# First heads of a decay attention loaded six tokens to a partition, two decay rows copied by the scalar engine, GpSimd's head constants in four steps, new constants of the planner

## The chip, the cores and the metric

The kernel runs on one core of one Trainium2 chip. The metric is device time in microseconds (us) of one execution, the median of several runs. A profiled execution of the kernel before, taken by the hardware profiler, gives the rows that are read below; its times count from the first instruction. The engines are named as the profile names them: PE (TensorE, matmuls), PEld (its weight loads), DVE (VectorE), ACT (ScalarE), POOL (GpSimd), SP (SyncE, which issues most DMAs). L903 is line 903 of the kernel before. In the changed kernel lines below the planner stand 5 to 20 lines further down, so that one statement has two numbers: L657 and L675 (scores), L763 and L781 (values), L903 and L921 (first MoE product), L804 and L822, L815 and L833 (the two matmul steps of a group's division).

## The reference

```python
# q, k, v: (8, 8, 576, 64); f: (8, 8, 576); all float32
scores = np.matmul(q, k.transpose(0, 1, 3, 2)) / np.sqrt(64)
cum = np.cumsum(np.log(np.clip(f, 1e-4, 1.0)), axis=-1)
scores = np.where(causal, -1e9, scores + cum[..., :, None] - cum[..., None, :])
attn = np.exp(scores - scores.max(-1, keepdims=True))
attn = attn / (attn.sum(-1, keepdims=True) + 1e-9)
x = np.matmul(attn, v).transpose(0, 2, 1, 3).reshape(8 * 576, 512)
h = np.maximum(np.maximum(x @ w1, x @ w2), x @ w3)      # 512 -> 768
out = h @ w_out                                        # 768 -> 512
```

## The kernel before

There are 64 heads, eight to a batch, and behind each batch the MoE product of its 576 tokens. The work of a head is cut into a unit 2 (queries 0 to 255) and a unit 1 (queries 256 to 575); for the first eight heads unit 1 is cut again into "a" and "b". Scores stand transposed, keys on partitions. `scores` (line 628) writes q times k and the causal mask into PSUM in a first pass (L657, L673), takes the maximum over keys with ACT and DVE (L712 to L724), across partitions with POOL (L727), lets POOL copy that row to where a matmul can use it (L734), subtracts it by a second pass of matmuls (L657 again) and lets ACT take the exponential (L742). `values` (line 752) multiplies by v and a column of ones (L763). For the first eight heads `finish_group` (line 790) divides four heads at once: PE turns the row sums (L804), DVE adds 1e-9 and takes the reciprocal (L819, L820), ACT widens them (L808), PE spreads them (L815). Later pairs of heads divide by way of two small DMAs through DRAM (`finish_pair`, line 863), and `split_x` makes the two parts of x that the MoE product needs (L877, L879). `gemm1` (L903) and `gemm2` (L932) are the MoE product in three fp32r products each; their weights are converted on the chip, 24 blocks, by ACT and DVE (`load_weights`, L511 to L521).

The first eight heads are prepared in another way than the rest. `load_raw` (line 459) loads a head's k and q, each as 96 partitions of six pieces of 64 numbers (256 bytes). `turn_head` (line 466) turns them by PE (L473) in two steps of three matmuls, and ACT and DVE copy the result out of PSUM into the tiles KF and QF (L479 to L482). Row 64 of KF holds the decays of the head's keys: `decay` (line 422) loads f, takes the logarithm and the running sum (L435), scales eight heads of it into a tile (L439), and ACT's queue issues one small DMA a head that puts one row into KF (L442). PE runs 20 matmuls on nothing (L455) beside this. When heads 0 to 3 are through, POOL writes constants into the tiles that the later heads use (`head_constants`, line 385, four memsets, one step for each of two buffers).

The order of all of it is worked out when the program is built, by a list scheduler (`Plan.emit`, line 86): every step has an engine, a cost and a priority, and each engine takes the ready step with the lowest rank, which is the step's priority less a share (`BLW`) of the work that hangs on it. Estimates of delays (`LAG`, `ROOM`, `LATE`, and `moved`, the time at which the queue of transfers is through) set when a step is ready; `LIKE` and `HOLD` say how far PE may go out of rank to put matmuls with 65 columns of weights behind a short one. What comes out is one fixed sequence for each engine, and on the chip each engine runs its own sequence in order, waiting at semaphores. The priorities are numbers at the end of the kernel function (lines 970 to 1051): `DP` for the decays, `DPW` for the weights' loads, `LEAD`, `UP`, `VO`, `FO`, `XO` for scores, values, division and split.

```python
add("POOL", 3300, lambda i=i: head_constants(i), w=[f"qs{i}", f"ks{i}"], prio=p)   # L1029
```

## Time and profile before

| | |
|---|---|
| median of 3 runs | 947.04 us (944.66, 947.04, 947.17) |
| the profiled execution, by the same clock | 944.31 us |
| its span, first to last instruction | 942.5 us |
| PE busy | 931.9 us (99%) |
| DVE, ACT, POOL busy | 641.0, 498.9, 249.8 us |
| mean granted clock of TensorE | 0.995 |

The span is 1.8 us shorter than the profiled execution's own time. A busy PE is not PE at its peak: a matmul counts as busy while it waits for its weights and while the clock is low. [...] "Idle before" in a row is the time in which that engine had nothing to do ahead of the row, with the instruction that ended the wait.

### The profile page before, as it was taken

How to read it: one execution, taken by the hardware profiler on the slowest of the kernel's cores; microseconds unless marked ns; L12 is line 12 of the kernel's file. 1: busy time of each engine (PE TensorE's matmuls, PEld its weight loads, DVE VectorE, ACT ScalarE, POOL GpSimd, SP SyncE). 2: the span in 40 equal slices, each digit the busy share in tenths (PEclk: the TensorE clock that was granted, in tenths of full speed). 3: DMA queues.
4: the chain of work that ended last, by engine and by line, in shares of the span. 5: the costliest groups of instructions: out<-in, count | busy, mean ns of one | idle time of the engine just before them, and what ended most of it. 6: DMA issues, size and time to landing. Idle time of an engine off the chain costs nothing.

```text
span 942.5 us, 18410 instructions
## 1 busy us (share of the span) xinstructions
PE 931.9 (99%) x6730; PEld 879.1 (93%) x6730; DVE 641.0 (68%) x1331; ACT 498.9 (53%) x1074; POOL 249.8 (27%) x313
## 2 busy tenths in 40 slices
PE   8999999999999999999999999999999999999998
PEld 6889988899989999999999999999999999999998
DVE  6998985567858686685967686686857776563311
ACT  5775754455555564555556564455655555453111
POOL 5663332322222221222122331222122321210000
PEclk9988999999999999999999999999999999999999
DMA  9776065546354354445445344545435454400000
GB/s 215 217 171 200 14 179 135 147 114 163 89 139 125 99 142 117 130 103 161 102 113 150 81 133 105 159 101 155 112 95 153 102 139 100 112 15 36 1 34 23
DMA packets 102826, 110.33 MB, mean 117 GB/s; under 512 B 60896, under 2 KB 70368, under 8 KB 102736
## 3 DMA queue, kind: packets, MB, share of 16 engines
q1 hardware_dynamic: 102480, 109.14, 44.7%
q8 instruction: 53, 0.87, 0.4%
q14 instruction: 37, 0.30, 0.1%
q10 hardware_dynamic: 256, 0.02, 0.0%
HBM read 49.56 MB, written 9.86 MB: 63 GB/s over the span
## 4 chain that ended last, share of the span: by engine, by line
PE 95%; DVE 2%; DMA 1%; ACT 1%; issue 0%; SPq 0%; ACTq 0%; DVEq 0%
PE mp L903 48%; PE mp L932 16%; PE t L763 15%; PE s L657 13%; DMA w<-in_moe_w_out_dram 1%; PE mp L473 0%; DMA qs<-u 0%; PE mp L657 0%; PE s L673 0%; SPq L578 0%; PE mp L763 0%; PE mp L815 0%; PE t L473 0%; PE t L815 0%; DVE w_r L521 0%
## 5 line engine op out<-in xcount | busy, mean ns | idle before, releaser
L903 PE MATMUL mp<-xh_r,w_r 128*128 128x320 f32 (+1 forms) x2160 | 466.4, 298 | 0.0
L903 PEld LDWEIGHTS mp<-xh_r,w_r 128*128 128x128 f32 x2160 | 357.2, 188 | 1.6 <-ACT tm L910 0.3
L903 PE MATMUL mp<-xl_r,w_r 128*128 128x320 f32 (+1 forms) x1080 | 319.5, 296 | 0.0
L727 POOL PARTITION_ALL_REDUCE gm<-mx x131 | 161.8, 1253 | 555.9 <-DVE mx L717 421.5
L903 PEld LDWEIGHTS mp<-xl_r,w_r 128*128 128x128 f32 x1080 | 203.3, 188 | 0.4
L912 DVE TENSOR_TENSOR tm<-mp,tm 128x256 f32<-128x256 f32 (+1 forms) x192 | 86.8, 452 | 87.1 <-PE mp L903 78.0
L742 ACT ACTIVATE pf<-s 128x384 f32<-128x384 f32 (+3 forms) x235 | 103.4, 508 | 53.7 <-PE s L657 48.4
L657 PE MATMUL s<-qs_r,ks_r 128*128 128x320 f32 (+4 forms) x784 | 123.7, 279 | 0.4 <-ACT hmh_r L915 0.4
L932 PE MATMUL mp<-w_r,hmh_r 128*128 128x512 f32 (+1 forms) x396 | 123.1, 393 | 0.0
L657 PEld LDWEIGHTS s<-qs_r,ks_r 128*128 128x128 f32 (+1 forms) x784 | 115.3, 181 | 5.3 <-ACT hmh_r L915 0.7
L749 DVE TENSOR_TENSOR pl_r<-pf,ph_r 128x1216 fp32r<-128x1216 f32 (+1 forms) x96 | 97.5, 1022 | 13.2 <-ACT ph_r L748 9.8
L717 DVE TENSOR_TENSOR mx<-mx,s 128x320 f32<-128x320 f32 (+3 forms) x248 | 92.1, 372 | 11.7 <-ACT mx L724 3.6
L748 ACT ACTIVATE ph_r<-pf 128x1216 fp32r<-128x1216 f32 (+1 forms) x96 | 83.0, 884 | 5.8 <-PE t L763 5.5
L915 ACT ACTIVATE hmh_r<-tm 128x256 fp32r<-128x256 f32 x96 | 39.7, 414 | 82.8 <-DVE tm L912 82.7
L932 PEld LDWEIGHTS mp<-w_r,hmh_r 128*128 128x128 f32 x396 | 70.3, 188 | 12.1
L534 DVE STREAM_TRANSPOSE hl<-hl 128x576 f32<-128x576 f32 x56 | 68.0, 1240 | 15.1 <-DMA hl<-in_k_dram 9.6
L932 PE MATMUL mp<-w_r,hml_r 128*128 128x512 f32 (+1 forms) x198 | 76.7, 387 | 0.0
L910 ACT ACTIVATE tm<-mp 128x256 f32<-128x256 f32 (+1 forms) x96 | 39.6, 413 | 59.1 <-PE mp L903 56.2
L917 DVE TENSOR_TENSOR hml_r<-tm,hmh_r 128x256 fp32r<-128x256 f32 x96 | 44.0, 458 | 24.7 <-ACT hmh_r L915 24.1
L734 POOL CAST qs_r<-gm 1x320 fp32r<-1x320 f32 (+1 forms) x112 | 56.0, 519 | 4.6
L763 PE MATMUL t<-ph_r,va_r 128*65 128x320 f32 (+4 forms) x336 | 52.7, 273 | 0.0
L763 PE MATMUL t<-ph_r,vl_r 128*65 128x320 f32 (+4 forms) x336 | 52.6, 273 | 0.0
(212 smaller groups left out, 1196.7 us busy)
## 6 DMA issues: line engine op xcount, KB each, us to landing
qs_r<-hl SPq DMA_DIRECT2D x168, 144.0 KB
ks_r<-hl SPq DMA_DIRECT2D x168, 144.0 KB
w<-in_moe_w_dram SPq DMA_DIRECT2D x18, 512.0 KB
out_dram<-o_r SPq DMA_DIRECT2D x35, 256.0 KB
hl<-in_q_dram SPq DMA_DIRECT2D x14, 576.0 KB
hl<-in_k_dram SPq DMA_DIRECT2D x14, 576.0 KB
r_r<-rdram SPq DMA_DIRECT2D x56, 144.0 KB
vn<-in_v_dram SPq DMA_DIRECT2D x50, 128.0 KB
```

Of the source, the lines that this page charges most:

```text
L534: add("DVE", 1085, lambda e=e, tt=tt, xs=xs: nc.vector.transpose(tt[:, e], xs[:, e]), [key + "0"], [key + "1"], prio)
L657: nc.tensor.matmul(bank[bk][0:l.shape[-1], col:col + w], l, rhs(qa, w), start=start and bk not in begun, stop=stop, skip_group_check=True)
L717: nc.vector.tensor_tensor(mt[:, a:a + w], mt[:, a:a + w], bank[bk][:, col:col + w], op=ALU.max)
L727: add("POOL", 450 + 2.6 * nq, lambda: nc.gpsimd.partition_all_reduce(gm, mt, P, bass.bass_isa.ReduceOp.max), [km, km + "a"], [kg], prio)
L734: add("POOL", 130 + 0.9 * nq, lambda: nc.gpsimd.tensor_copy(shift_row(), gm[row:row + 1, :]), [kg], [kx], prio)
L742: add("ACT", act_cost(w), lambda bk=bk, w=w, col=col: nc.scalar.activation((pg(unit) if pk else pf)[:, col:col + w], bank[bk][:, 0:w], AF. ...
L748: add("ACT", act_cost(PW[unit]) + 40, lambda: nc.scalar.activation(ph(unit), pf, AF.Copy), [fk], [hk], prio)
L749: add("DVE", dve_cost(PW[unit]), lambda: nc.vector.tensor_tensor(pl(unit), pf, ph(unit).bitcast(F32), op=ALU.subtract), [fk, hk], [lk], prio)
L763: nc.tensor.matmul(t[:D + 1, qa:qa + w], src()[:, j, c, :], pr()[:, col:col + w], start=first and x == 0, stop=last, skip_group_check=True,)
L903: nc.tensor.matmul(m, unit_w(i, fb)[:, w, kt, :], xx, start=kt == 0 and x == 0, stop=kt == KT - 1 and x == 2,)
L912: add("DVE", dve_cost(cn), lambda m=m: nc.vector.tensor_tensor(t, m, t, op=ALU.max), [km, kt_], [kt_], prio)
L932: nc.tensor.matmul(mp[:, 0:cn], l[:, fb, cs], unit_o(fb)[:, r, ds], start=fb == 0 and x == 0, stop=fb == FT - 1 and x == 2,)
```

## The change

Heads 0 to 7: a partition now takes six tokens that follow each other, so k and q are 96 pieces of 1,536 bytes each; a step of `turn_head` turns q alone or k alone, so q's can begin before k is there; the copies out of PSUM put the tokens back in order, writing every sixth number. f is loaded first of all, with head 1's row a second time on partition 64, and ACT copies the rows of heads 0 and 1 itself; six rows stay small DMAs. The first three blocks of weights are loaded ahead of heads 2 to 7. POOL's constants are eight steps. The maximum and what follows on DVE and POOL stand half a priority earlier (`CB`). The planner has one queue of transfers for all engines, a longer delay for ACT and DVE, and other priorities.

```diff
-    ROOM = {"PE": (0.93, 0), "ACT": (1.0, 0), "DVE": (1.0, 0), "POOL": (1.0, 450), "SP": (1.0, 0)}
-    LIKE, HOLD = 1.7, 1.0
+    ROOM = {"PE": (0.93, 0), "ACT": (1.0, 0), "DVE": (1.0, 60), "POOL": (1.0, 450), "SP": (1.0, 0)}
+    MORE = (0, 150, 0, 0, 0)
+    LIKE, HOLD = 3.0, 0.55
...
-    def head_constants(i):
-        nc.gpsimd.memset(KS(i)[:, :, S:SP].bitcast(F32), 0.0)
...
+    def head_constants(i, prio):
+        for key, ns, go in (
+            (f"ks{i}", 380, lambda: nc.gpsimd.memset(KS(i)[:, :, S:SP].bitcast(F32), 0.0)),
+            (f"qs{i}", 1100, lambda: nc.gpsimd.memset(QS(i)[96:P, :, :].bitcast(F32), 1.0)),
...
+            add("POOL", ns, go, w=[key], prio=prio)
...
-        dma(ft, fs, w=["pf1"], prio=DP)
+        dma(ft, fs, w=["pf1/0"], prio=DP)
+        dma(fx[BH:BH + 1], fs[1:2], w=["pf1/1"], prio=DP, bytes_=2304)
...
+        for n in range(2):
+            add("ACT", act_cost(S), lambda n=n: nc.scalar.activation(
+                KF[n][D:D + 1, :], fx[BH * n:BH * n + 1, :], AF.Copy, scale=-1.0 / scale), ["pf1"], [f"kf{n}/2"], DP)
...
-        for n in range(H):
+        for n in range(2, H):
             add("ACT", 600, lambda n=n: nc.scalar.dma_start(out=KF[n][64:65, :], in_=c8[n:n + 1, :]),
...
-                out=RAWQK[n][:, :, c, :], in_=src[b, h].rearrange("(a p) d -> p a d", p=96)),
+                out=RAWQK[n][:, c], in_=src[b, h].rearrange("(p x) d -> p (x d)", p=96)),
...
+        for c, buf, kc in ((0, QF, "qf"), (1, KF, "kf")):
...
-            add("PE", 3 * (4 * 96 / 2.4 + 5), go, [f"raw{n}/0", f"raw{n}/1", "idf"], [kp], prio, rows=96)
+            add("PE", 3 * 225, go, [f"raw{n}/{c}", "idf"], [kp], prio, rows=96)
+            dst = buf[n][0:D, :].rearrange("d (p a e) -> d e a p", a=3, e=2)
+            for e in range(2):
+                src = ps[D * e:D * e + D, 0:288].rearrange("d (a p) -> d a p", a=3)
...
-        add("DVE", cm, most, kp, [km], prio)
+        add("DVE", cm, most, kp, [km], prio - CB)
...
-    DP = -8.0
-    DPW = 3.0
+    DP = -9.6
+    DPW = -8.0
...
-    UP, VO, FO, XO = -1.5, 1.0, -1.0, -1.8
+    UP, VO, FO, XO = 0.25, 0.95, -0.05, -1.9
```

The order that comes out differs nearly everywhere; three places matter below.

**ACT at the start.** Before, from the logarithm (L432) to the copies of head 1 (qs_65 and qs_66 are the tiles of heads 0 and 1, u_91 the tile of scaled decays):

```order
L432 ACTIVATE pf_80<-pf_80 64x576
L482 ACTIVATE qs_65<-mp_130 64x288
L434 ACT_TABLE_LOAD
L434 ACTIVATE tm_122<-tm_122 1x1
L481 ACTIVATE qs_65<-mp_130 64x288
L482 ACTIVATE qs_66<-mp_131 64x288
L442 DMA qs_65<-u_91 1x16x36
L442 DMA qs_66<-u_91 1x16x36
L442 DMA ks_67<-u_91 1x16x36
L442 DMA ks_68<-u_91 1x16x36
L482 ACTIVATE qs_66<-t 64x288
```

And now:

```order
L443 ACTIVATE pf_80<-pf_80 65x576
L445 ACT_TABLE_LOAD
L445 ACTIVATE tm_122<-tm_122 1x1
L498 ACTIVATE qs_65<-mp_129 64x3x96
L450 ACTIVATE qs_65<-pf_80 1x576
L450 ACTIVATE qs_66<-pf_80 1x576
L456 DMA ks_67<-u_91 1x16x36
L456 DMA ks_68<-u_91 1x16x36
L498 ACTIVATE qs_65<-mp_130 64x3x96 x2
```

The rows of heads 0 and 1 are copies, and the copies of head 0's k (from mp_130) stand behind two issues of DMAs.

**POOL at the head constants.** Before (gm_84 is the maximum of a unit "a" or "b", ph_71 the row that the second pass uses, ks_r and qs_r the tiles of the later heads):

```order
L386 MEMSET ks_r 128x2x64
L388 MEMSET qs_r 32x1152
L389 MEMSET ks_r 32x2x576
L390 MEMSET ks_r 1x640
L727 ISA gm_84<-mx_82 128x160 x2
L734 CAST ph_71<-gm_84 1x160 x2
L386 MEMSET ks_r 128x2x64
```

And now:

```order
L745 ISA gm_84<-mx_82 128x160
L393 MEMSET ks_r 128x2x64
L752 CAST ph_71<-gm_84 1x160
L395 MEMSET ks_r 32x2x576
L393 MEMSET ks_r 128x2x64
L745 ISA gm_84<-mx_82 128x160
L396 MEMSET ks_r 1x640
L752 CAST ph_71<-gm_84 1x160
```

Before, the row of the first maximum is copied only after the second maximum; now each is copied after its own.

**PE at the division of heads 4 to 7, unit 2.** Before, from the turn to the second spread (s_124 to s_126 are the score banks of unit 1, xh the tiles of heads 4 and 5):

```order
L804 MATMUL mp_131<-hdl,ph_79 128x4 x2
L657 MATMUL s_124<-ph_71,pl_72 128x160 x3
L657 MATMUL s_124<-ph_71,pl_72 128x32
L815 MATMUL mp_131<-hdl,rx 128x128 x2
L657 MATMUL s_125<-ph_71,pl_72 128x160 x3
```

And now:

```order
L822 MATMUL mp_131<-hdl,ph_79 128x4 x2
L675 MATMUL s_125<-ph_71,pl_72 128x160 x3
L675 MATMUL s_126<-ph_71,pl_72 128x160
L675 MATMUL s_126<-ph_71,pl_72 128x64
L822 MATMUL t<-hdl,ph_79 107x4 x2
L822 MATMUL t<-hdl,ph_79 106x4
L675 MATMUL s_125<-xh 128x160 x3
L833 MATMUL mp_131<-hdl,rx 128x128 x2
```

Ten matmuls stand between turn and spread, where there were four, and the next turn (into t) is among them.

## Rows read from the trace of the kernel before

**Rows 1.** The page, part 1: busy us (share of the span) and instructions of PE.

```profile
PE 931.9 (99%) x6730; PEld 879.1 (93%) x6730; DVE 641.0 (68%) x1331; ACT 498.9 (53%) x1074; POOL 249.8 (27%) x313
```

**Rows 2.** Stretches of 2 us: length, busy us by engine, PEclk, DMA share, GB/s.

```profile
62.00:64.00 2.00, 1.45 (x11) 1.15 (x9) 1.93 (x4) 1.55 (x4) 1.96 (x3) 1.00 1.05 209
64.00:66.00 2.00, 0.93 (x6) 0.84 (x7) 2.00 (x6) 1.28 (x3) 1.94 (x4) 0.95 1.07 209
66.00:68.00 2.00, 2.00 (x8) 1.63 (x8) 1.90 (x5) 1.91 (x5) 1.94 (x3) 0.50 1.13 192
...
76.00:78.00 2.00, 2.00 (x21) 1.96 (x18) 1.36 (x5) 0.35 (x1) 1.06 (x2) 0.99 1.04 306
```

**Rows 3.** Timeline around the division of heads 4 to 7: PE's rows (start us, us).

```profile
62.97 0.61 PE L804 MATMUL mp<-hdl,ph 97*128 97x4 f32 x4
64.10 0.61 PE L657 MATMUL s<-ph,pl 1*128 1x160 f32 x4 [0.52 <-POOL ph L734]
65.68 1.13 PE L815 MATMUL mp<-hdl,rx 128*128 128x128 f32 x4 [0.97 <-ACT rx L808]
```

**Rows 4.** Timeline of the same stretch: DVE's rows.

```profile
64.52 0.16 DVE L819 TENSOR_SCALAR hdl<-mp 128x8 f32<-128x8 f32 x1
```

**Rows 5.** Timeline of the same stretch: POOL's rows.

```profile
57.51 1.29 POOL L727 PARTITION_ALL_REDUCE gm<-mx  x1 [0.16 <-POOL ks_r L390]
62.04 1.37 POOL L727 PARTITION_ALL_REDUCE gm<-mx  x1 [3.24 <-DVE mx L717]
63.30 1.48 POOL L734 CAST ph<-gm 1x160 fp32r<-1x160 f32 x2
```

**Rows 6.** Timeline of the first 15 us: PE's rows.

```profile
10.08 1.48 PE L473 MATMUL mp<-hdl,w 96*128 96x96 f32 x12
11.39 1.46 PE L455 MATMUL s<-ident 128*128 128x512 bf16 x6
14.20 0.89 PE L657 MATMUL s<-qs 128*128 128x256 f32 x4 [1.35 <-DMA qs<-u]
```

**Rows 7.** Timeline of the first 15 us: DVE's and ACT's rows (ACTq issues DMAs).

```profile
5.04 1.15 DVE L418 MEMSET xl<- 64x576 f32 x2
6.21 0.45 DVE L430 TENSOR_SCALAR pf<-pf 64x576 f32<-64x576 f32 x1
7.42 1.35 DVE L435 TENSOR_TENSOR_SCAN pf<-pf 64x576 f32<-64x576 f32 x1 [0.38 <-ACT pf L432]
9.04 1.13 DVE L439 TENSOR_SCALAR u<-pf 8x576 f32<-8x576 f32 x1
...
10.21 1.24 ACTq L442 DMA_DIRECT2D qs<-u  x2
12.77 0.41 ACT L482 ACTIVATE qs<-t 64x288 f32<-64x288 f32 x1 [2.74 <-DVE ks L479]
```

**Rows 8.** Stretch of 2 us while the first heads are loaded, columns as in rows 2.

```profile
10.00:12.00 2.00, 2.00 (x17) 1.66 (x16) 1.90 (x5) 0.03 (x1) 0.00 (x0) 1.00 1.38 203
```

**Rows 9.** Timeline of PE: scores of unit 1 with and without values in between.

```profile
307.19 0.57 PE L657 MATMUL s<-qs_r,ks_r 128*128 128x320 f32 x4
307.60 0.78 PE L763 MATMUL t<-ph_r,va_r 128*65 128x64 f32 x5
...
315.90 0.81 PE L657 MATMUL s<-qs_r,ks_r 128*128 128x320 f32 x5
...
439.73 0.31 PE L903 MATMUL mp<-xh_r,w_r 128*128 128x320 f32 x1
439.88 0.31 PE L903 MATMUL mp<-xl_r,w_r 128*128 128x320 f32 x1
...
441.49 0.75 PE L763 MATMUL t<-ph_r,va_r 128*65 128x64 f32 x5
```

**Rows 10.** Timeline at the last batch: the last values, and the last split of x.

```profile
848.68 0.34 PE L763 MATMUL t<-pl_r,va_r 128*65 128x128 f32 x2
...
862.97 0.76 DVE L879 TENSOR_TENSOR xl_r<-u,xh_r 128x576 fp32r<-128x576 f32 x1 [0.75 <-ACT xh_r L877]
```

More of the change, by code (lines that the diff above doesn't have):

```diff
@@ L106, in emit @@
                 heapq.heappush(wait[s[0]], (0.0, i))
-        done, moved = 0, {}
+        done, moved = 0, 0.0
         short = 0.0
@@ L141, in emit @@
             if self.steps[i][5]:
-                moved[e] = max(moved.get(e, 0.0), end + 650) + self.steps[i][5]
-                end = moved[e] + self.LATE
+                if self.steps[i][5] < 50 and e == "ACT":
+                    end += 1850
+                else:
+                    end = moved = max(moved, end + 650) + self.steps[i][5]
+                end += self.LATE
             for u in users[i]:
@@ L146, in emit @@
                 lag = self.LAG["SP" if self.steps[i][5] else e][self.ENGINES.index(self.steps[u][0])]
-                lag = 0 if same and e == "PE" else lag
+                lag = 0 if same and e == "PE" else lag + self.MORE[self.ENGINES.index(self.steps[u][0])]
                 ready[u] = max(ready[u], end + lag)
@@ L411 @@
     nc.gpsimd.load_library(next(x for x in all_libraries if any(c.__name__ == "InstPartitionAllReduce" for c in x.instructions)))
-    add("POOL", 1060, sums_constants, w=[f"rs{g}{u}" for g in range(2) for u in (1, 2)], prio=0.0)
+    add("POOL", 1060, sums_constants, ["cs"], [f"rs{g}{u}" for g in range(2) for u in (1, 2)], 0.0)
     add("POOL", 1100, constants, w=["const"], prio=-9)
@@ L478, in turn_head @@
-            if x == 0:
-                add("DVE", dve_cost(288), lambda ps=ps, cs=cs: nc.vector.tensor_copy(QF[n][0:D, cs], ps[0:D, 0:288]), [kp], [f"qf{n}/{x}"], prio)
-            else:
-                add("ACT", act_cost(288), lambda ps=ps, cs=cs: nc.scalar.activation(QF[n][0:D, cs], ps[0:D, 0:288], AF.Copy), [kp], [f"qf{n}/{x}"], prio)
-            add("ACT", act_cost(288) + 115, lambda ps=ps, cs=cs: nc.scalar.activation(KF[n][0:D, cs], ps[D:P, 0:288], AF.Copy), [kp], [f"kf{n}/{x}"], prio)
+            add("PE", 3 * 225, go, [f"raw{n}/{c}", "idf"], [kp], prio, rows=96)
@@ new lines, in turn_head @@
+            dst = buf[n][0:D, :].rearrange("d (p a e) -> d e a p", a=3, e=2)
+            for e in range(2):
+                src = ps[D * e:D * e + D, 0:288].rearrange("d (a p) -> d a p", a=3)
+                if c == 0 and e == 0:
+                    add("DVE", dve_cost(288), lambda dst=dst, src=src: nc.vector.tensor_copy(dst[:, 0], src), [kp], [f"{kc}{n}/0"], prio)
+                else:
+                    add("ACT", act_cost(288) + 115 * e, lambda dst=dst, src=src, e=e: nc.scalar.activation(
+                        dst[:, e], src, AF.Copy), [kp], [f"{kc}{n}/{e}"], prio)
@@ L505, in load_weights @@
         else:
-            dma(cols(raw), src.bitcast(I32)[:, :, 2 * c0:2 * c1], after, [key], prio=DPW + 0.01 * step, bytes_=524288)
+            add("SP", 560, lambda: nc.sync.dma_start(out=cols(raw), in_=src.bitcast(I32)[:, :, 2 * c0:2 * c1]),
+                after, [key], DPW + 0.01 * step, 524288 / 360)
             pair = raw.rearrange("p (x t) -> p x t", t=2)
@@ L734, in scores @@
         add("POOL", 130 + 0.9 * nq, lambda: nc.gpsimd.tensor_copy(
-            shift_row(), gm[row:row + 1, :]), [kg], [kx], prio)
+            shift_row(), gm[row:row + 1, :]), [kg], [kx], prio - CB)
         sc = scale if first else 1.0
@@ L967, in moe @@
                 done += 18 * mm_cost(512, P)
-    LEAD, MLAG, WP, WR = 2.0, 0.5, 0.0, 0.5
-    DP = -8.0
-    DPW = 3.0
+    LEAD, MLAG, WP, WR = 1.95, 0.2, 0.0, 0.6
+    DP = -9.6
+    DPW = -8.0
     warm_up()
     decay()
-    QP = -0.2
+    QP = -0.4
     UO = 1
-    LO = -1.0
-    UP, VO, FO, XO = -1.5, 1.0, -1.0, -1.8
-    HP, VP = -0.4, 0.2
+    LO = -0.95
+    UP, VO, FO, XO = 0.25, 0.95, -0.05, -1.9
+    HP, VP = -1.4, 0.5
+    HC, VO1, XO1, QP1, CB = 0.0, 1.0, -2.95, -0.1, 0.45
     order = (1, 2) if UO else (2, 1)
     for n in range(H):
-        load_raw(n, n - 9)
+        load_raw(n, n - 9.0)
     for n in range(H):
-        turn_head(n, n - 5)
+        turn_head(n, n - 5.5)
         if n % 2 == 0:
             load_v(n // 2, n - LEAD - VP)
-    for unit, up in ((2, 0.0), (1, 0.7)):
+    for unit, up in ((2, 0.0), (1, 1.0)):
         for n in range(H):
@@ L993 @@
             for x in subs:
-                values(n, x, p + VO)
+                values(n, x, p + VO1)
             if n % 4 == 3:
@@ L1028 @@
         retire([f"qf{i + 2}", f"kf{i + 2}"], [f"ks{i}"])
-        add("POOL", 3300, lambda i=i: head_constants(i), w=[f"qs{i}", f"ks{i}"], prio=p)
+        head_constants(i, p + HC)
     for n in range(H, BH):
@@ L1036 @@
         if n % 4 == 0:
[L1037 removed]
+            load_quad(b, h // 4, p - (QP1 if b < 2 else QP))
         if n % 2 == 0:
```

40 lines of the change are left out of this document (19 added, 21 removed).

## Prediction

> **What bounds the kernel now.** The first view is the page's list of engines: PE is busy 99% of the span, DVE 68%, ACT 53% [rows 1]. So time can come from three places only: the few microseconds in which PE stands still, stretches with a low clock, and matmuls that take longer than they need because of what stands beside them. Next come the stretches of 2 us with their granted clock. It is 1.00 nearly everywhere; from 66 to 76 us five rows in a row show 0.50, the lower of the two levels, with 0.95 ahead of them and 0.99 behind [rows 2]. In those 10 us PE is busy and does half the work, which costs 5.0 us, and the two rows beside add 0.12: 5.1. Then the timeline just ahead of the fall, for what PE did there: a wait of 0.52 us at 64.10 for the row that POOL casts, a step, and a wait of 0.97 at 65.68 for the row sums that ACT widens [rows 3]. The timelines of DVE and POOL say why those came late [rows 4, 5]. Last come the first 15 us, where the first scores start at 14.20 after a wait of 1.35 for the DMA with the decays [rows 6], and the last batch, where x goes over DRAM.
>
> The profiled execution took 944.31 us and the span is 942.5; the sum is made against 944.31. The median of the runs shown is 947.04, 2.7 above it, and the fastest run 944.66. I add nothing for that difference and leave it to the range. About 0.3%, 2.8 us, is what a measurement of this kernel can tell from no change, so "the same" is 944.2 to 949.9.
>
> **The opening.** Before, DVE reaches the clip of f (L430) at 6.21, behind the tiles' memsets; two of them take 1.15, one 0.58 [rows 7]. Now f is the first load and three memsets fewer stand ahead of the clip, 1.7 us. But two memsets, 1.15, stand between clip and running sum, where 0.76 lay before (6.66 to 7.42). So the sum over f starts 1.7 - 0.4 = 1.3 us earlier and ends at about 7.4 where it ended at 8.77 [rows 7].
>
> Behind it the old way was a scaling on DVE (1.13), an issue on ACT's queue (two take 1.24), the DMA's own flight and the wait of 1.35 on PE [rows 6, 7]. The new way for head 0 is all on ACT's queue: 0.27 as between the running sum's end and the next instruction before, two row copies, two issues of DMAs (1.24), and two copies of k out of PSUM (0.41 each). No row shows a copy of one partition by 576. A copy of 288 columns took 0.41 [rows 7], so it lies between 0.41 and twice that, 0.82; it has twice the columns but starts only once, so I take 0.7, nearer the upper end. Together 0.27 + 1.4 + 1.24 + 0.82 = 3.7 and the first scores at 11.1, 3.1 us earlier than 14.20; with the two bounds 10.5 to 11.4. Not all of that is won. Of the seven groups of three turns that stood ahead of the first scores, three now stand behind them. Twelve matmuls of that kind, two groups of a head's both halves, take 10.08 to 11.39 [rows 6], 0.66 for six of them, which is one group's work; 3 x 0.66 = 2.0 is only moved. The opening gives **-1.1**.
>
> What could spoil it is the loads: three blocks of weights, 1.57 MB, are issued ahead of heads 2 to 7. With f and heads 0 and 1 (0.74 MB) and head 2's q (0.15 MB) that is 2.46 MB before head 2 can be turned. The pieces of 256 bytes moved at 203 GB/s [rows 8], by which this takes 12.1 us; a stretch with larger pieces moved at 306 [rows 2], by which it takes 8.0. Head 2 is wanted at about 11.9, behind the first scores of 0.89: by 306 nearly 4 us are left for the start and the flight of the first load, by 203 none, and head 2 comes late by what these take, an estimated 3 us. Both kinds of loads now have larger pieces (1,536 bytes and more), so I take 306 and no cost, and keep the 3 us for the range.
>
> The turned copies have the same number of columns, 288, and now write every sixth number of KF and QF. Before they took 0.41 on ACT with numbers side by side [rows 7]. No row of before shows a stride, so the price lies between nothing and a second 0.41 for each; I take nothing, since columns and partitions are as many as before and only the places of the writes differ; rival B holds the other end. [...]
>
> **The hole at 62 to 66 us.** This is the largest term. POOL has the first maximum at 57.51 + 1.29 = 58.80, then does constants and waits 3.24 us for DVE's second maximum at 62.04, and casts both rows together from 63.30 [rows 5]. PE wanted the first of them and waited 0.52 [rows 3]. In the new order each row is cast behind its own maximum, one memset between, so the first row is there some 4 us earlier; with `CB` DVE's maxima also go ahead of other work. The 0.52 goes. Cover behind it: the second row is then the later one, and it stays at 62.04 or earlier, as long as the long subtraction of 1.34 [rows 4] isn't put ahead of it.
>
> The wait of 0.97 is for the division. From the end of L804 (62.97 + 0.61 = 63.58) through DVE (L819 at 64.52) and ACT to L815 at 65.68 is 2.1 us [rows 3, 4]. Four matmuls of 160 columns stood under it, 0.61. Now ten stand under it, 0.15 each by the same row, 1.5. What is left is 2.1 - 1.5 = 0.6, or nothing if DVE is free and L819 doesn't come 0.94 after its input. I take 0.6.
>
> With 1.49 of waits within 1.6 us turned into one of 0.6, I let the clock stay at 1.00. That is the choice on which most of the sum hangs; rival A is the other. The term is 0.52 + 0.97 + 5.1 - 0.6 = **-6.0**.
>
> **The order of the scores of unit 1.** A unit 1 has a short matmul of 64 columns in its fourth block of keys. Five such matmuls took 0.81 us where four of 320 columns alone took 0.57, so the short one costs 0.24; a plain step of 320 takes 0.15 [rows 9]: 0.09 more where the next matmul has 128 columns of weights to load. Where values with their 65 columns follow, this is hidden in part, and the values behind a short one take 0.78 for five where they take 0.75 behind others [rows 9], 0.03 back. So one place without values costs 0.06. The old order has 73 short ones followed by 128 columns, the new one 95: 22 x 0.06 = **+1.3**, and between nothing and 2.0 (22 x 0.09).
>
> **The last batch.** The last values end at 848.68 + 0.34 = 849.02, and the last part of x is there at 862.97 + 0.76 = 863.73, over DRAM [rows 10]: 14.7 us, in which 88 matmuls of the MoE product covered PE before. In the new order 76 stand there; twelve of 320 columns at 0.15 (439.73 to 439.88 [rows 9]) are 1.8 us. The 88 lasted 15.6, the 76 last 13.8: 14.7 - 13.8 = **+0.9**, from nothing to 1.8.
>
> Work that goes unpriced: the changes of `LIKE`, `HOLD`, `LEAD` and the rest move DVE's and ACT's work, under PE's cover with DVE at 68% [rows 1]; the loads and conversions of weights for later batches come ahead of their use as before. If that cover were gone at one place it would cost one wait of about 1 us, as the 0.97 of [rows 3].
>
> **The sum.** -1.1 - 6.0 + 1.3 + 0.9 = -4.9, and 944.31 - 4.9 = **939.4 us**. The bounds: opening -1.8 to +1.9 (with late loads), hole -6.6 to -5.4, scores 0 to 2.0, last batch 0 to 1.8; taken together 936 to 944, and the median's 2.7 above the profile may add to that.
>
> **Rivals.** *A: the hole moves and the clock falls anyway.* The waits ahead of the division are only shifted, and the clock falls behind them as it did at 66. For it speaks that the division's chain is as long as before and that a wait for DVE can take the place of that for POOL. Against it speaks the order, which puts ten matmuls under the chain. The other terms remain: 939.4 + 6.0 = 945.4, no change that can be told.
>
> *B: the copies with a stride are slow.* If each takes 0.82, the two copies of head 0's k add 0.8 ahead of the first scores, and 18 copies of heads 2 to 7 on ACT add 7.4 us there, of which PE, that has other work for two thirds, waits for 2.5: 939.4 + 3.3 = 942.7. For it speaks that nothing in the trace excludes it; against it, that the number of writes is the same, and that ACT has room for some of it (53% [rows 1]). [...]
>
> *C: slower.* The next turn (into t) now stands between turn and spread, and its reciprocal needs DVE too. If DVE has the 1.34 us of L540 [rows 4] in front of it, both spreads wait, each with a fall of the clock. The hole stays and a second one like it comes, 0.52 + 0.97 + 5.1 = 6.6: 939.4 + 6.0 + 6.6 = 952.0. It decides from the point where DVE takes up the sums over 0.9 us later than PE has turned them, about the 0.94 of before [rows 3, 4]. Against it speaks `CB`, which moves DVE's maxima only by half a priority and doesn't put the subtraction first.
>
> **How the numbers follow.** The forecast gets 0.63, A 0.17, B 0.12, C 0.08. The forecast's own range is 935 to 943. The range reaches over A and B and leaves out C and the ends of the forecast: 934.0 to 947.5. Faster by over 0.3% are the forecast and B, less 0.03 for those of their upper ends that lie over 944.2: 0.72. Within 0.3% lie A and that 0.03: 0.20. Slower is C: 0.08.
>
> **What would show it.** In the profile after: no row with PEclk 0.50 behind 60 us (a row of 0.50 there is A, two stretches C); POOL's first cast within 2 us of its maximum; PE's first scores at 10.5 to 11.4, with a row copy of 576 between 0.41 and 0.82; ACT's copies of 64x3x96 at 0.41 (0.8 is B); a wait of PE of at most 0.6 at the division; a rate near 306 GB/s from 4 to 12 us; and a wait of about 1 us ahead of the last pair's MoE product. The prediction is wrong if the time before 60 us is longer than before, or if waits show up in batches 2 to 7, where I priced none.

## The result, and the profile after

The changed kernel takes 949.47 us (median of 22 runs, 943.27 to 956.53), the kernel before, run beside it as often, 945.27 (941.43 to 947.25). The ratio is 1.0049 (95% interval 1.0027 to 1.0072): slower by about half a per cent, where 939.4 was forecast. The spread is part of the result: by the mean granted clock of TensorE the 22 runs fall into three groups, five at 1.000 (943.27 to 945.70), eleven at 0.993 to 0.995 (947.34 to 950.08) and six at 0.986 (954.53 to 956.53). The profiled execution, 956.53 us, is one of the last, so it shows the loss at its largest; it is the only one of them that was profiled. Runs below that count as slow are left out of the ratios, though not of the medians: it concerns one of 12 with the copies alone (without it 946.59) and one of 12 with the queue undone (944.30).

The first view is the page's list of engines of the kernel after; it answers to [rows 1].

```profile
PE 944.7 (99%) x6730; PEld 890.3 (93%) x6730; DVE 644.0 (67%) x1331; ACT 513.3 (54%) x1076; POOL 245.0 (26%) x313
```

PE has 12.8 us more of busy time for the same 6,730 matmuls, and its idle time is no larger. Matmuls have become longer, which points to the clock. The stretches of 2 us answer to [rows 2] and [rows 8] (same columns).

```profile
2.00:4.00 2.00, 2.00 (x6) 0.68 (x5) 1.65 (x5) 0.22 (x2) 1.74 (x6) 1.00 0.72 206
...
8.00:10.00 2.00, 2.00 (x11) 1.87 (x10) 1.79 (x4) 1.23 (x2) 1.87 (x3) 1.00 1.07 355
...
14.00:16.00 2.00, 0.42 (x2) 0.00 (x0) 0.00 (x0) 0.11 (x1) 0.00 (x0) 1.00 0.51 141
16.00:18.00 2.00, 0.66 (x2) 0.61 (x3) 0.00 (x0) 1.96 (x4) 0.00 (x0) 0.65 0.64 184
18.00:20.00 2.00, 2.00 (x11) 1.85 (x10) 0.62 (x2) 1.13 (x2) 0.07 (x1) 0.50 0.83 206
...
42.00:44.00 2.00, 2.00 (x8) 1.67 (x8) 0.71 (x3) 1.69 (x3) 0.00 (x0) 0.52 0.67 211
...
66.00:68.00 2.00, 2.00 (x14) 1.75 (x14) 1.56 (x5) 1.48 (x4) 1.18 (x2) 1.00 0.00 0
```

The entries of the granted clock in this trace and in that of before hold two values alone, 1.00 and 0.50. From 18 to 42 us all twelve rows stand at 0.50 and the next at 0.52: 12.0 + 0.96 = 13.0 us lost (the row at 0.65, in which PE stood for the most part, isn't counted), where before the lower level lasted from 66 to 76 and cost 5.1. That old fall is gone (66 to 68 at 1.00, as are the rows behind it). By these rows the clock alone is +7.9 of the 12.2 us between the two profiled executions. What PE did ahead of the new fall stands in the timelines of the first 20 us: PE's rows, then those of ACT and of the queues that issue DMAs (ACTq, SPq). The matmuls on nothing that PE runs beside the loads (L469) are called warm-ups from here on.

```profile
9.72 4.70 PE L469 MATMUL s<-ident 128*128 128x512 bf16 x13
17.34 1.62 PE L675 MATMUL s<-qs 128*128 128x256 f32 x4 [2.92 <-issue]
```

```profile
3.67 1.53 SPq L525 DMA_DIRECT2D w<-in_moe_w_dram  x3
...
7.15 0.69 ACT L498 ACTIVATE qs<-mp 64x288 f32<-64x288 f32 x1
...
7.86 1.37 ACT L450 ACTIVATE qs<-pf 1x576 f32<-1x576 f32 x2
...
10.87 0.31 SPq L476 DMA_DIRECT2D w<-in_q_dram  x1
...
14.19 1.65 ACTq L456 DMA_DIRECT2D ks<-u  x2
14.45 0.31 SPq L476 DMA_DIRECT2D w<-in_k_dram  x1
...
15.89 0.67 ACT L498 ACTIVATE qs<-mp 64x288 f32<-64x288 f32 x1 [6.65 <-DMA w<-in_q_dram]
```

ACT is done with both row copies at 9.23. The next thing in its order is an issue of a DMA, head 2's row. Its input has been there since 9 us, but it goes out at 14.19. In the trace's records each of the DMAs of this stretch reports its landing on one of eight counters (semaphores 100 and 102 to 108), taken over in turn over all queues. The first eight issues wait for none; from the ninth on (the third block of weights, at 4.69) each waits until the DMA that had its counter before has landed: SP's issues at 9.29, 10.87 and 14.45 go out 0.02 us behind the last parts on 107, 108 and 102 (9.27, 10.85, 14.43). Head 2's row took over counter 100 from the third block of weights, whose last part landed at 14.12. So ACT stood for 4.96 us, the copies of head 0's k behind the issue with it, and PE, out of warm-ups at 14.42, stood 2.92 us. The 1.65 us of the row are two issues, 0.62 and 0.54, and 0.49 between them, in which the second stood for head 3's q (counter 104). SP's queue stands in the same way from 11.18 to 14.45, for head 2's q.

The division of heads 4 to 7 answers to [rows 3, 4]:

```profile
83.69 0.51 PE L822 MATMUL mp<-hdl,ph 97*128 97x4 f32 x4
84.13 0.74 PE L675 MATMUL s<-ph,pl 1*128 1x160 f32 x5
84.52 0.15 DVE L837 TENSOR_SCALAR hdl<-mp 128x8 f32<-128x8 f32 x1
...
84.94 0.72 PE L822 MATMUL t<-hdl,ph 97*107 97x4 f32 x6
...
85.53 1.08 PE L675 MATMUL s<-xh 128*128 128x160 f32 x6
85.94 0.41 ACT L826 ACTIVATE rx<-hdl 128x256 f32<-128x256 f32 x1
86.45 0.66 PE L833 MATMUL mp<-hdl,rx 128*128 128x128 f32 x4
```

The chain from the turn's end (84.20) to the spread (86.45) is 2.25 us, as long as the 2.1 of before, and the matmuls in between cover all of it: the spread has no wait.

The first MoE product of the third and of the last batch, before and after, bound the steady part:

```profile
329.15 0.33 PE L903 MATMUL mp<-xh_r,w_r 128*128 128x256 f32 x1
...
860.79 0.31 PE L903 MATMUL mp<-xh_r,w_r 128*128 128x320 f32 x1
```

```profile
339.87 0.33 PE L921 MATMUL mp<-xh_r,w_r 128*128 128x256 f32 x1
...
872.89 0.31 PE L921 MATMUL mp<-xh_r,w_r 128*128 128x320 f32 x1
...
873.45 0.76 DVE L897 TENSOR_TENSOR xl_r<-u,xh_r 128x576 fp32r<-128x576 f32 x1 [0.81 <-ACT xh_r L895]
```

The difference is 10.7 us at the third batch and 12.1 at the last: 1.4 us arise in between, and 10.7 ahead.

### The profile page after: what moved, and what is told of

It reads as the page before. It is cut to its first block, busy times and chain, and to the rows that moved or that the text cites. A ratio compares the mean times of both kernels' runs of the same rounds, so it can differ in the third digit from the quotient of the medians.

```text
span 954.7 us, 18537 instructions
## 1 busy us (share of the span) xinstructions
PE 944.7 (99%) x6730; PEld 890.3 (93%) x6730; DVE 644.0 (67%) x1331; ACT 513.3 (54%) x1076; POOL 245.0 (26%) x313
## 3 DMA queue, kind: packets, MB, share of 16 engines
q1 hardware_dynamic: 94802, 109.14, 43.6%
## 4 chain that ended last, share of the span: by engine, by line
PE 98%; ACT 1%; issue 0%; DVE 0%; POOL 0%; POOLq 0%; ACTq 0%; DVEq 0%
PE mp L921 48%; PE mp L950 16%; PE t L781 15%; PE s L675 13%; PE mp L488 2%; PE s L469 1%; PE mp L675 1%; PE t L488 1%; PE mp L781 1%; PE s L691 0%; PE t L833 0%; ACT hl L556 0%; ACT pf L760 0%; PE mp L833 0%; DVE mx L735 0%
## 5 line engine op out<-in xcount | busy, mean ns | idle before, releaser
L921 PE MATMUL mp<-xh_r,w_r 128*128 128x320 f32 (+1 forms) x2160 | 473.1, 297 | 0.2 <-DVE tm L930 0.2
L760 ACT ACTIVATE pf<-s 128x512 f32<-128x512 f32 (+3 forms) x235 | 106.7, 505 | 89.8 <-PE s L675 86.8
L675 PE MATMUL s<-qs_r,ks_r 128*128 128x320 f32 (+4 forms) x784 | 130.1, 283 | 0.0
L675 PEld LDWEIGHTS s<-qs_r,ks_r 128*128 128x128 f32 (+1 forms) x784 | 117.4, 181 | 6.8 <-issue 0.2
L767 DVE TENSOR_TENSOR pl_r<-pf,ph_r 128x384 fp32r<-128x384 f32 x96 | 95.9, 999 | 27.1 <-ACT ph_r L766 24.8
L766 ACT ACTIVATE ph_r<-pf 128x384 fp32r<-128x384 f32 x96 | 83.9, 874 | 29.0 <-PE t L781 28.2
L935 DVE TENSOR_TENSOR hml_r<-tm,hmh_r 128x256 fp32r<-128x256 f32 x96 | 42.0, 438 | 28.2 <-ACT hmh_r L933 27.5
L752 POOL CAST qs_r<-gm 1x256 fp32r<-1x256 f32 (+1 forms) x112 | 51.5, 460 | 7.2
L781 PE MATMUL t<-pl_r,va_r 128*65 128x320 f32 (+4 forms) x336 | 52.4, 272 | 0.0
```

What stands on the lines that cost most here:

```text
L675: nc.tensor.matmul(bank[bk][0:l.shape[-1], col:col + w], l, rhs(qa, w), start=start and bk not in begun, stop=stop, skip_group_check=True)
L752: add("POOL", 130 + 0.9 * nq, lambda: nc.gpsimd.tensor_copy(shift_row(), gm[row:row + 1, :]), [kg], [kx], prio - CB)
L760: add("ACT", act_cost(w), lambda bk=bk, w=w, col=col: nc.scalar.activation((pg(unit) if pk else pf)[:, col:col + w], bank[bk][:, 0:w], AF. ...
L766: add("ACT", act_cost(PW[unit]) + 40, lambda: nc.scalar.activation(ph(unit), pf, AF.Copy), [fk], [hk], prio)
L767: add("DVE", dve_cost(PW[unit]), lambda: nc.vector.tensor_tensor(pl(unit), pf, ph(unit).bitcast(F32), op=ALU.subtract), [fk, hk], [lk], prio)
L781: nc.tensor.matmul(t[:D + 1, qa:qa + w], src()[:, j, c, :], pr()[:, col:col + w], start=first and x == 0, stop=last, skip_group_check=True,)
```

## The experiments

Three theories stood: **Q**, ACT's in-order queue stands at the issues of DMAs; **L**, the weights ahead of heads 2 to 7 make those heads' loads late; **S**, the copies that write every sixth number are slow. All but the loop's and the queue's edits move finished steps of the planner's list and change no other engine's sequence, so a difference belongs to what was moved. Each version was profiled once. Times are medians of 12 runs (6 for the early weights in the kernel before), ratios against runs of the kernel before on the same chip; [a; b] is the 95% interval. The ratio goes by all of these runs and not by the medians: where a few runs are long, a median under that of the kernel before and a ratio over 1 can stand together. Versions measured on different chips are better compared by their ratios.

**Issues behind the copies** (ACT's order):

```diff
-L456 DMA ks_67<-u_91 1x16x36
-L456 DMA ks_68<-u_91 1x16x36
 L498 ACTIVATE qs_65<-mp_130 64x3x96 x2
-L456 DMA xh<-u_91 1x16x36
 L498 ACTIVATE qs_66<-mp_131 64x3x96
 L498 ACTIVATE qs_66<-t 64x3x96 x2
+L456 DMA ks_67<-u_91 1x16x36
+L456 DMA ks_68<-u_91 1x16x36
+L456 DMA xh<-u_91 1x16x36 x2
```

> The changed kernel with one thing moved: ACT issues the small DMAs of heads 2 to 5 (L456) behind the copies of heads 0 and 1 (L498) instead of between them. Everything else keeps its order. Theory Q (the queue): the wait of 2.92 us ahead of the first scores is ACT's, whose queue stood from 9.23 to 14.19 at the issue of head 2's row because the DMA counter it takes over still belonged to the third block of weights. Then the first scores come at 10.7 to 11.5 instead of 17.34 and no PE wait over 1 us is left before 20 us; the long stretch at 0.50 goes and the median falls to about 943. Theory L (the loads): heads 2 to 7 are late because 1.57 MB of weights go ahead of them. Then the first scores come at 11 too, but PE stands 2 to 3 us at the turn of head 2 (L488), which can't begin before about 14.4, and the stretch at 0.50 stays; median 947 to 950.

944.04 us, ratio 1.0014 [0.9986; 1.0042]. From its timeline:

```profile
10.74 0.89 PE L675 MATMUL s<-qs 128*128 128x256 f32 x4 [0.22 <-issue]
...
13.27 2.51 PE L488 MATMUL mp<-hdl,w 96*128 96x96 f32 x18 [1.53 <-DMA w<-in_q_dram]
...
14.12 1.85 ACTq L456 DMA_DIRECT2D ks<-u  x2
...
17.63 0.67 ACT L498 ACTIVATE ks<-mp 64x288 f32<-64x288 f32 x1 [5.09 <-DMA ks<-u]
```

The first scores come at 10.74, so Q is right about them (what the clock has to do with it stands in the last section). The issue goes out at 14.12, for head 3's q (counter 104): ACT computes nothing for 5.09 us, some 2.1 of them issuing and 2.9 standing, only behind head 1's copies now. L is right too: head 2's q is late, PE waits 1.53, and another 1.29 at 18.36 for a copy of ACT. Three of the 12 runs still take 951 to 955 us.

**Weights behind head 7's loads** (SP's order: the three issues of L525 move behind the last of L476):

> The changed kernel with one thing moved: the three blocks of weights are loaded behind head 7's q and k instead of ahead of head 2's. Both theories expect the first scores at 11 to 12 and head 2 turned right behind them: theory Q because the issues on ACT's queue then take over counters of small loads that have long landed, theory L because the loads of heads 2 to 7 are in time. No stretch at 0.50 before 60 us; median 939.5 to 943, where the changed kernel's runs without any fall of the clock stand at 943.3 to 944.2. If the median stays at 947 or more, both are wrong and something else in the order makes the wait.

944.58 us, ratio 0.9995 [0.9970; 1.0019].

```profile
10.94 1.63 ACTq L456 DMA_DIRECT2D ks<-u  x2
...
14.06 0.89 PE L675 MATMUL s<-qs 128*128 128x256 f32 x4 [3.15 <-issue]
```

The expectation missed: with small loads as predecessors the issue still waits, until 10.94, and the first scores come at 14.06, behind a wait of 3.15. No lower level follows that wait before 43.6 us. SP's queue runs ahead with its loads (a k goes out at 10.87), and ACT's issue stands behind them: ACT computes nothing for 3.36 us, some 1.6 of them issuing, and the timeline puts the wait down to a load of k.

**Both moves:**

> The changed kernel with both moves: weights behind head 7's loads, and ACT's issues of heads 2 to 5 behind the copies of heads 0 and 1. Theory Q: like the one with the weights late, or 0.5 to 1.2 us better, since two issues of 0.62 us no longer stand ahead of head 0's k. Theory L: the same as the one with the weights late. First scores 10.5 to 11; median 939 to 943.

948.64 us, ratio 1.0033 [1.0004; 1.0061]; a miss. First scores at 10.73, but now ACT stands at the issue of head 6's row, for a block of weights (2.71 us of standing and 0.55 of issuing), and PE waits 2.86 until 19.8. Each repair on ACT's queue moves the stop to its next issue.

**The kernel before with early weights** (its three issues ahead of head 2's):

> The kernel before with one thing moved: its three blocks of weights are loaded ahead of heads 2 to 7, as in the changed kernel. Theory L: PE waits 2 us or more at the turn of head 2 (L473) at about 10, since the loads then take until 14; the first scores come 2 to 5 us later than 14.20 and the clock falls behind them; 948 to 956. Theory Q: ACT's six issues of decay rows (L442) take over the counters of the weights' blocks and stand up to 5 us, the first scores (which need such a row) come at 17 to 19, and the clock falls; 950 to 956. If it comes out within 0.3% of the kernel before, the early weights are not the cause.

952.04 us, ratio 1.0075 [1.0052; 1.0099]. From its list of PE's waits (us in total, times, longest):

```profile
PE mp L473 <- DMA w<-in_q_dram: 5.4, 1, 5.4
```

The early weights alone cost the kernel before 7 us, by L's route: PE waits for head 2's loads, and the first scores come at 21.75. ACT's first two issues go out at 10.21 as in the kernel before, so its queue isn't what made it late.

**Rows on SP's queue:**

```diff
-            add("ACT", 600, lambda n=n: nc.scalar.dma_start(out=KF[n][64:65, :], in_=c8[n:n + 1, :]),
+            add("ACT", 600, lambda n=n: nc.sync.dma_start(out=KF[n][64:65, :], in_=c8[n:n + 1, :]),
```

> The changed kernel with the six small DMAs of decay rows (L456) issued by SP's queue instead of ACT's, at the same places of the order. Theory Q says that only the queue they stand in matters: ACT has no issue to stand at, so the first scores come at 10.7, as when the issues stood behind the copies, and ACT's copies of heads 1 to 3 are never held up by a DMA. Theory L says that the early weights still hold up head 2's q: PE waits 1.5 us at the turn of head 2, as it did there, and more if SP now stands at a row. Median 942 to 945 with Q alone true; falls of the clock behind the 1.5 us in some of the runs.

942.75 us, ratio 0.9974 [0.9952; 0.9997]: one line turns the change from slower into faster. ACT stands at no issue. PE's wait was 1.1 us for head 1's k near 7 us, with the clock at 0.50 behind it from 8 to 14, so that the first scores came at 14.86 and not 10.7 in the profiled execution.

**And the weights behind head 7:**

> The same, and the three blocks of weights loaded behind head 7's q and k. With theories Q and L both true no PE wait over 1 us stands before 40 us but for the start; the median is 941 to 943 and the spread of the runs narrows to some 3 us, since no wait is left for the clock to fall behind in the opening. A third theory, S: the copies out of PSUM (L496, L498) take 0.68 instead of 0.41, because each write goes 24 bytes on; ACT then is the bound of the opening, and PE waits 0.5 to 1.5 us for copies of heads 2 to 4 even here.

945.52 us, ratio 1.0008 [0.9986; 1.0029]; a miss. First scores at 10.71 and head 2 in time, but further on:

```profile
21.44 0.68 ACT L529 ACTIVATE w<-w 128x512 f32<-128x512 f32 x1 [2.21 <-DMA w<-in_moe_w_dram]
...
25.01 0.91 PE L488 MATMUL mp<-hdl,w 96*128 96x96 f32 x6 [2.73 <-DVE xh L496]
```

ACT waits for the weights it is to convert, heads 5 to 7 wait behind that, and the clock falls at 26 us. Weights too early kept PE waiting for head 2's q (1.53 us with the issues behind the copies), weights too late stopped ACT (2.21).

**And the copies in the order of the writes:**

```diff
-            dst = buf[n][0:D, :].rearrange("d (p a e) -> d e a p", a=3, e=2)
+            dst = buf[n][0:D, :].rearrange("d (p a e) -> d e p a", a=3, e=2)
...
-                src = ps[D * e:D * e + D, 0:288].rearrange("d (a p) -> d a p", a=3)
+                src = ps[D * e:D * e + D, 0:288].rearrange("d (a p) -> d p a", a=3)
```

> The same as the one before, and the copies out of PSUM run over the tokens in the order in which they are written: each write goes 8 bytes on instead of 24, each read of PSUM 384 bytes. Theory S: if it is the step of the writes that costs, ACT's and DVE's copies of 64x288 fall from 0.68 to 0.40 to 0.50, PE waits less for them, and the median is 1 to 2 us under the one before. If the reads of PSUM cost as much, they stay at 0.68 or rise, and the time is the same or up to 2 us longer.

942.88 us, ratio 0.9982 [0.9961; 1.0002]. Groups by line and shape, of the run ahead of it and of this one (the mean of one in ns follows the comma):

```profile
L498 ACT ACTIVATE qs<-mp 64x288 f32<-64x288 f32 x4 | 2.7, 682 | 0.1
```

```profile
L498 ACT ACTIVATE qs<-mp 64x288 f32<-64x288 f32 x4 | 1.7, 426 | 0.3 <-DVE qs L496 0.3
```

S is right: 0.68 us with steps of 24 bytes, 0.43 with steps of 8, 0.41 side by side [rows 7]. The reads of PSUM, 384 bytes apart now, cost nothing that shows. PE doesn't wait less for it, as was expected: its wait of 2.73 for ACT stays, with 2.96 at 25.20, since ACT waits for the weights as before.

**The cast alone, in the kernel before:**

> The kernel before with one thing moved: behind the first set of head constants POOL casts the row of the first maximum right after that maximum (L727, L734) instead of after the second. Theory of the prediction: PE's wait of 0.52 us for POOL at 64.10 goes, the wait of 0.97 for the division stays or grows by up to 0.5. If the two together brought the clock down from 66 to 76 us, it stays up and the median falls by 2 to 5 us, to 940 to 943. If the wait for the division alone does it, the clock falls as before and the median stays within 1 us of the kernel before.

946.91 us, ratio 1.0020 [1.0001; 1.0039].

```profile
63.95 0.61 PE L804 MATMUL mp<-hdl,ph 97*128 97x4 f32 x4
...
64.98 0.69 DVE L517 SCALAR_TENSOR_TENSOR hdl<-w,hdl 128x512 int32<-128x512 int32 x1
65.59 0.16 DVE L819 TENSOR_SCALAR hdl<-mp 128x8 f32<-128x8 f32 x1
...
67.26 0.71 PE L815 MATMUL mp<-hdl,rx 128*128 128x128 f32 x4 [2.16 <-ACT rx L808]
```

The 0.52 us for POOL is not saved but paid at the division, where the wait grows from 0.97 to 2.16, by more than the 0.5 expected. The clock falls behind it again, from 69.2 to 76.0, and a shorter fall stands at 48.7 to 52.1.

**All three mends** (rows on SP, copies in the order of the writes, and the weights one by one):

```diff
 L476 DMA w_115<-in_k_dram 96x384
+L525 DMA w_95<-in_moe_w_dram 128x4x256
...
 L476 DMA w_116<-in_k_dram 96x384
+L525 DMA w_96<-in_moe_w_dram 128x4x256
...
 L476 DMA w_117<-in_k_dram 96x384
+L525 DMA w_97<-in_moe_w_dram 128x4x256
```

> The changed kernel with three mends: the rows of decays issued by SP's queue, the copies out of PSUM in the order in which they are written, and the three blocks of weights loaded one by one behind heads 4, 5 and 6. Theories Q, L and S together: first scores at 10.7, head 2 turned without a wait over 0.5 us, ACT not kept waiting over 1 us for a block of weights at 20 to 24 us, so no PE wait over 1 us before 50 us but for the start. The steady part costs 1.0 to 1.3 us more than in the kernel before. Median 938.5 to 941, near the 939.4 forecast for the change, and few runs with a fall of the clock. If the weights still come late for ACT, a PE wait of 1 to 3 us is left at 22 to 26 us and the median is 941 to 943.

939.89 us (937.12 to 941.20), ratio 0.9943 [0.9921; 0.9966]: faster than both kernels. Its list of PE's waits over the first 140 us (same columns):

```profile
PE s L469 <- POOL ident masks.py:199: 1.5, 1, 1.5
PE mp L921 <- ACT tm L928: 1.0, 2, 0.5
PE s L675 <- ACT pf L760: 0.4, 2, 0.3
PE t L781 <- ACT ph L796: 0.3, 1, 0.3
```

No wait over 0.5 us but that at the start, and a granted clock of 1.00 in every stretch of 2 us there, though the stretches ahead of 13.5 us rest on no record. Only the first scores, at 14.55 in the profiled execution, came later than expected (the last section says why).

**The copies alone, in the changed kernel:**

> The changed kernel with only the copies out of PSUM run in the order of the writes. Theory S would save 24 x 0.26 us on ACT in the opening; theory Q says that ACT's queue still stands from 9 to 14 us at the issue of head 2's row, so that the first scores come at 16 to 17 and the clock falls as in the changed kernel. Median 946 to 950 by Q, under 944 if the copies were the main cause.

946.78 us, ratio 1.0003 [0.9977; 1.0029]; first scores at 16.82 behind a wait of 3.5. Not the main cause, as Q said.

**More cover in the kernel before:**

> The kernel before with POOL's cast moved up, and the first spread of the division of heads 4 to 7 (L815) put behind nine more matmuls of scores and their masks, the second behind the next values; what hangs on them moves with them. With the cast alone the wait there was 2.16 us and the clock fell behind it. Theory of the prediction: the matmuls are the cover, about 1.5 us of them, so a wait of 0.3 to 0.8 us is left. If the clock then stays at 1.00 behind 60 us, the median is 941 to 943.5; if it falls all the same, it stays at 945 to 947.

946.92 us, ratio 1.0029 [1.0007; 1.0051]; a miss.

```profile
64.04 0.61 PE L804 MATMUL mp<-hdl,ph 97*128 97x4 f32 x4
...
67.99 2.24 PE L657 MATMUL s<-xh 128*128 128x160 f32 x8 [2.15 <-ACT pf L742]
```

The added matmuls write a bank that ACT must read first, and ACT reads it behind the same conversions of weights. PE waits as long, one step further on.

**Two mends, the weights early:**

> The changed kernel with the rows of decays on SP's queue and the copies in the order of the writes, and the weights ahead of heads 2 to 7 as in the change. Against the one with the rows on SP alone (942.75) it tells what the copies are worth where no DMA stops ACT: theory S says 0.5 to 2 us, 941 to 942.5; nothing if PE waits for the loads of heads 1 and 2 there. Theory L: waits of about 1 us for these loads are left at 6 to 14 us.

941.20 us, ratio 0.9980 [0.9953; 1.0008]; first scores at 10.20, a wait of 1.72 for head 2's q left, by L. In the profiled execution, 948.16, the lower level stands behind it from 15.2 to 35.7 us.

**The queue undone, the copies undone:**

> The version with three mends, with the rows of decays (L456) back on ACT's queue. Theory Q: ACT stands again at the issues of heads 2 to 7, for loads that are smaller now, so 1 to 4 us in all ahead of the copies of heads 0 to 3; PE waits 1 to 3 us ahead of the first scores, and the clock falls behind it in some of the runs; median 941 to 946. If the queue were no cause once the weights stand further back, the median stays at 939.5 to 940.5.

> The version with three mends, with the copies out of PSUM writing every sixth number again. Theory S: each takes 0.68 again, ACT has 24 x 0.26 = 6.2 us more to do before 32 us, and PE waits 0.5 to 1.5 us for copies of heads 2 to 7; median 940.5 to 943. If ACT has room for it, the median stays within 0.5 us of 939.9.

944.73 us, ratio 1.0006 [0.9978; 1.0034], and 941.36, ratio 0.9957 [0.9935; 0.9979]. From the version with all three the queue is worth 4.8 us by the medians, the copies 1.5, and the early weights (the experiment ahead) 1.3; by the ratios, as each version ran on its chip, it is 6.0, 1.3 and 3.5. Only for the queue do the intervals lie apart, so the sizes of the other two are not shown. With the queue undone the mechanism is Q's, ACT standing 2.88 us at its second issue (10.60 to 13.48) for a block of weights; but in the profiled execution PE waits only 0.56 for it ahead of the first scores (14.98) and 0.50 at 20.7, not the 1 to 3 us expected, since its warm-ups took until 14.4.

**The division first, in the kernel before:**

> The kernel before with POOL's cast moved up, and with the division's steps put ahead of the conversions of weights: on DVE L819 and L820 ahead of L517 and L513, on ACT L808 and L742 ahead of L520. With the cast alone PE waited 2.16 us for L808. The conversions stand for some 0.65 (L517) + 0.3 (L513) + 0.4 (L520) of the chain. If they are what makes the hole, PE waits 0.3 to 1.0 us there, the stretch at 0.50 from 66 to 76 us shrinks or goes, and the median falls to 940 to 943.5; if not, the wait stays near 2 and the median at 945 to 947.

944.46 us, ratio 0.9987 [0.9965; 1.0009].

```profile
66.80 0.61 PE L804 MATMUL mp<-hdl,ph 97*128 97x4 f32 x4
67.73 0.16 DVE L819 TENSOR_SCALAR hdl<-mp 128x8 f32<-128x8 f32 x1
...
68.63 0.71 PE L815 MATMUL mp<-hdl,rx 128*128 128x128 f32 x4 [0.68 <-ACT rx L808]
```

The chain shrinks from 2.70 us (64.56 to 67.26 with the cast alone) to 1.22, the wait to 0.68, and no fall follows it at 66 to 76. The median, over the 940 to 943.5 expected, is 2.5 us under that of the cast alone on another chip (by the ratios 3.1), though one wait of 0.9 at the second spread and one of 1.4 at the MoE product have come up, and a fall from 51.5 to 54.9. In the kernel before, most of the hole was the conversions of weights standing ahead of the division on DVE and ACT.

## Why the prediction was wrong

- **The opening, forecast -1.1: the step that failed.** "Two issues of DMAs (1.24)" was priced as issuing time alone. Issuing took 1.16 us, but 5.45 of standing came with it, and the first scores came at 17.34, not 11.1; by the comparison in the last section 2.8 of these 6.2 us are the stop, and most of the rest is PE's low rate until 13.2 us, which no term or rival held. The rest of that chain held within a microsecond: without the issues it gives 11.1 - 1.24 = 9.9, and with the issues out of the way the first scores come at 10.74, 10.73, 10.71, of which 0.5 are the slower copies and 0.2 a running sum that ended at 7.60, not 7.4. The rows of before show no such stop (their four issues, from 10.21 to 12.7, follow each other without a gap; the first two stand in [rows 7]); I asked what was queued behind an issue, and not what the issue itself waits for.
- **The loads.** "I take 306 and no cost": the rate was nearly right and the cost wrong. From 4 to 12 us 290 GB/s were moved on average (205 to 355 in stretches of 2 us). Even so head 2's q landed at 14.43 (SP's issue at 14.45 waited for it), late by 2.5 us, near the 3 us of the other bound (an estimate with no row beside it; in the trace of before the last part of the first load lands at 3.40 us). In the trace's records each load lands in sixteen parts: fifteen of head 2's q were there at 12.09, the last at 14.43, and of the third block of weights fifteen at 11.47, the last at 14.12. So in this execution one late part set both the stop of ACT and that of SP; in that of the version with two mends, with the same early weights, all of the block was there at 12.28 and of the q at 12.81. What delays a part is not shown.
- **The clock.** "I let the clock stay at 1.00" holds where it was said, behind the division. No rival let a fall come in the opening, where a wait of 2.92 us now stands; it cost 13.0 us in the profiled execution, and 5 of the 22 runs show none (1.000). Those five have a median of 943.95, so by an estimate 5.5 us of the median of 949.47 are falls, and 4.6 over the forecast stand without any.
- **The copies.** "I take nothing" was wrong and rival B's mechanism real: 0.27 us more a copy, two thirds of the 0.41 that it priced. With 24 bytes from write to write a copy takes 0.68 us, with 8 bytes 0.43, side by side 0.41; why 24 cost and 8 hardly do is not shown. In the version with all three mends it is worth 1.5 us of the whole by the medians, which is not clear of the noise.
- **The hole, forecast -6.0: right.** Both waits and the fall at 66 to 76 us are gone: 0.52 + 0.97 + 5.1 = 6.6 from rows. That the later fall is not just the earlier one moved, the versions show: in none of the twelve profiled executions of the changed kernel and its versions does the level drop between 60 us and the last three, with or without a fall in the opening, while in four of five of the kernel before and its versions it drops behind the division, in all but the one with the division first. The ten matmuls lasted all of the chain's 2.25 us where 1.5 was worked out, so that the 0.6 left over wasn't there. The cause of the chain in the kernel before was not named: it is as long as it is because of the conversions in it. (The 1.34 us of L540 is not among the rows under [rows 4]; the trace of before has it at 55.20.)
- **The steady order, forecast +1.3: right,** +1.4 from the third batch to the last. The mechanism is there too. Counted in the two traces, in that stretch 47 short matmuls were followed by 128 columns of weights before and 69 are now, 22 more, and such a short one with the matmul of 320 columns behind it takes 0.26 us in both kernels.
- **The last batch, forecast +0.9: wrong.** The difference is 12.1 us at its start, and the spans differ by 12.2. The last x was there at 874.21, 12.2 us behind the last values (862.00), where 14.7 was carried over from before; the shorter cover was enough.

With all three mends the change takes 939.89, where 939.4 was forecast. That is not the forecast come true: the terms were priced as if these three costs did not exist.

## What to carry to other kernels

An issue of a DMA isn't only its issuing time. Here one of 0.62 us stood 4.96 us for a counter that an older, larger transfer still held, until the last of its sixteen parts had landed, and ACT's copies behind it waited too. With these issues on SP's queue, which does no computing in this kernel, the ratio to the kernel before was 0.9974 and not 1.0049; keep such issues on a queue that does nothing else. Before a large load is put ahead of small ones, look up who issues next and what that issue takes over. And compare the sizes of steps in an access, not only its number of columns: here the same reordering cost 0.27 us a copy in one order of loops and 0.02 in the other.
